# Products before copies in the token-major query units of a linear-attention and MLP kernel, with two buffer names changed

## The chip, the core and the metric

The kernel runs on one core of a Trainium2 chip. The metric is device time in microseconds (us) for one execution, the median of several. Five engines take part, each with its own instruction stream that it works off in order: TensorE (PE, with its weight loads as PEld), VectorE (DVE), ScalarE (ACT), GpSimd (POOL) and SyncE (SP, which issues the DMAs here).

## What is computed

Linear attention over 8 batches of 8 heads (576 tokens, 64 dimensions, 128 features), then a two-layer MLP over all 4608 tokens:

```python
def phi(x):
    proj = x @ w_phi                                  # 64 -> 128
    proj = proj - max(abs(proj), axis=-1)
    return concat([exp(proj), exp(-proj)], axis=-1)   # 256 features
kv  = phi(k).T @ v
z   = sum(phi(k), over tokens)
num = phi(q) @ kv
den = phi(q) @ z + 1e-6
x   = num / den                  # per head; heads side by side: 4608 x 512
h   = x @ w_in                   # 512 -> 2048
out = max(0.01 * h, h) @ w_out   # 2048 -> 512
```

## The kernel before

**Pairs.** Two heads are worked on together: 32 pairs, four for each batch. Pairs 0 to 3 (batch 0) go through `first_k_phase` and `first_q_phase` at the start. All others are a stream, `attention()`, in which the key phase of pair i (`k_phase`) alternates with the query phase of pair i-1: `token_q_phase` for pairs 4 to 7 (batch 1) and `q_phase` from pair 8 on.

**A token-major query unit.** A unit is up to 256 tokens of a pair (`units`: 256, 256 and 64). `q_group` (pairs 4 to 7, 12 units) and the inner loop of `first_q_phase` (nine units) do the same: PE projects the queries, DVE takes the largest magnitude and subtracts it, PE transposes the result, and ACT takes two exponentials (L322 and L323, in the first units L523 and L524). Then, for each of the two heads j, PE multiplies with the key-value sums (L328, L538) and ACT copies the numerator to `ring` (L330, L541) and the denominator plus 1e-6 to `dn` (L331, L542). DVE transposes `dn`, inverts it and transposes it back, and POOL multiplies. [...] A product is two matrix instructions, and the profile shows each f32 instruction of this kind as two records: so four instructions and eight records per unit of 256 tokens.

**Buffers.** `st(shape, type, tag)` takes a tile from a pool in which each tag has one buffer, or two for the tags in `BUFS` (`eq` among them). Who asks next for a tag in the program gets the buffer when the one before has been released. The key-value sums of a pair (`kvh`, L282 to L284) are copied by ACT out of the PSUM tile of tag `c`, of which there is one.

**Weights.** `load_weights` brings the MLP's weights in 32 pieces (w_in and w_out for each of 16 slices of the hidden layer, 512 KB each) through two staging buffers. For each piece: DMA, ACT L159, DVE L160, L161, L162, ACT L164 (into the scratch tile `cr`, whose tag is `kvl`), DVE L165, ACT rounds it (L68, `w0h` or `w1h`), DVE subtracts (L73, `w0l` or `w1l`). The stage's buffer is free for the next DMA when L162 and L164 have read it. From pair 8 on the tag `kvl` also holds the low part of the key-value sums.

**MLP.** Blocks of 256 tokens, 18 of them, each with 16 slices: `layer1` (12 matrix instructions of 256 columns, L590, L591, L593) and `layer2` (six of 512 columns, L609 to L611), in pure f32r, three products for one. The slices of block 0 come while the weights are still being made.

**The order.** Nothing of it is written by hand. Every instruction carries a priority from its place in the source, and a scheduler with an estimate of times sorts each engine's instructions ahead of the run. The key phases and units are generators, so that the stream goes on between two slices. A small edit can so change the order on all engines.

Of the kernel before, what the change touches and what calls it, by code (L numbers as in the profile page):

```python
# [9 lines left out]
F32 = mybir.dt.float32  # L10
# [3 lines left out]
AF = mybir.ActivationFunctionType  # L14
# [3 lines left out]
P = 128  # L18
B, H, S, D = 8, 8, 576, 64
NP = H // 2  # L20
F = 128
U = 288
DM = 512
# [22 lines left out]
def attention_moe_kernel(ctx: ExitStack, tc: tile.TileContext, q, k, v, vt, w_phi, w_in, w_out, out):  # L46
    nc = tc.nc
# [7 lines left out]
    def st(shape, dt, tag):  # L55
        return sp.tile(shape, dt, tag=tag, name=tag, bufs=BUFS.get(tag, 1))
# [8 lines left out]
    def copy_(key, o, i):  # L65
        e = pick(key) or "a"
        if e == "a":
            nc.scalar.copy(o, i)  # L68
        else:
            (nc.vector if e == "v" else nc.gpsimd).tensor_copy(o, i)  # L70
# [4 lines left out]
    def pt(tag):  # L75
        return ps.tile([P, 512], F32, tag=tag, name=tag, bufs=PBUFS[tag])
# [113 lines left out]
    def k_phase(i):  # L190
# [22 lines left out]
        for g in range(3):  # L213
            w = 2 if g < 2 else 1
# [4 lines left out]
            if plain:  # L219
                pk = pt("a")  # L220
                for s in range(w):
                    t0 = (2 * g + s) * P if g < 2 else S - P
                    proj(pk, s, rk[:, t0 : t0 + P])
                pkv = pk[r, 0 : 256 * w].rearrange("p (a f) -> p a f", f=F)
            else:
                for s in range(w):
                    t0 = (2 * g + s) * P if g < 2 else S - P
# [5 lines left out]
                    x = pmk[r, 2 * s : 2 * s + 2]  # L233
# [45 lines left out]
            for t in range(2):  # L279
                nc.tensor.transpose(kvtv[:, j, t], kvs[:, j, t], ident[0:66, 0:66])  # L280
        if i < NN:
            kvh = st([P, 2, 2, P], F32, "kvh")  # L282
            nc.scalar.copy(kvh[:, :, :, 0:64], kvtv[:, :, :, 0:64])
            nc.scalar.copy(kvh[:, :, :, 64:P], kvtv[:, :, :, 64:65].broadcast_to([P, 2, 2, 64]))  # L284
            kvs_of[i] = kvh, None
        else:
            kvh = st([P, 2, 2, P], F32R, "kvh")
            kvl = st([P, 2, 2, P], F32R, "kvl")
            zb = kvtv[:, :, :, 64:65].broadcast_to([P, 2, 2, 64])
            copy_("kvh", kvh[:, :, :, 0:64], kvtv[:, :, :, 0:64])  # L290
            copy_("kvh", kvh[:, :, :, 64:P], zb)
            nc.vector.tensor_tensor(kvl[:, :, :, 0:64], kvtv[:, :, :, 0:64], kvh[:, :, :, 0:64].bitcast(F32), op=ALU.subtract)
            nc.vector.tensor_tensor(kvl[:, :, :, 64:P], zb, kvh[:, :, :, 64:P].bitcast(F32), op=ALU.subtract)
            kvs_of[i] = kvh, kvl
# [5 lines left out]
    def proj(pk, s, x, n=P):  # L300
        nc.tensor.matmul(pk[0:n, 256 * s : 256 * s + 256], lhsT=x, rhs=bd, start=True, stop=True)  # L301

    def q_group(rq, t0, w, kvh, x, pm, dn):
        pq = pt("a")
        ns = max(w // P, 1)
        n = min(w, P)
        for s in range(ns):
            c = slice(t0 + s * P, t0 + s * P + n)
            proj(pq, s, rq[:, c], n)
        m4 = st([P, 4], F32, "m4")  # L310
        pqv = pq[0:n, 0 : 256 * ns].rearrange("p (a f) -> p a f", f=F)
        nc.vector.tensor_reduce(m4[0:n, 0 : 2 * ns], pqv, axis=AX.X, op=ALU.max, apply_absolute_value=True)
        nc.vector.tensor_tensor(pm[0:n, 0 : 2 * ns], pqv,
                                m4[0:n, 0 : 2 * ns].unsqueeze(2).broadcast_to([n, 2 * ns, F]), op=ALU.subtract)
        yield
        tr = pt("a")[:, 0 : 2 * w].rearrange("p (j t) -> p j t", j=2)
        for s in range(ns):
            for j in range(2):
                nc.tensor.transpose(tr[:, j, s * P : s * P + n], pm[0:n, 2 * s + j], ident[0:n, 0:n])
        ee = [st([P, 2, U], F32, "eq").rearrange("p a b -> p (a b)")[:, 0 : 2 * w].rearrange("p (j t) -> p j t", j=2)  # L320
              for t in range(2)]
        nc.scalar.activation(ee[0], tr, AF.Exp)  # L322
        nc.scalar.activation(ee[1], tr, AF.Exp, scale=-1.0)  # L323
        yield
        nm = pt("a")[:, 0 : 2 * w].rearrange("p (j t) -> p j t", j=2)
        for j in range(2):
            for t in range(2):
                nc.tensor.matmul(nm[:, j], lhsT=kvh[:, j, t], rhs=ee[t][:, j], start=t == 0, stop=t == 1)  # L328
            rr = slice(64 * j, 64 * j + 64)
            nc.scalar.copy(x[rr], nm[0:64, j])  # L330
            nc.scalar.activation(dn[rr], nm[64:128, j], AF.Copy, bias=1e-6)  # L331
        yield
        dt = st([P, U], F32, "mb")[:, 0:w]
        nc.vector.transpose(dt, dn)
        rc = st([P, 9], F32, "rc")[:, 0 : w // 32]
        nc.vector.reciprocal(rc, dt.rearrange("p (a c) -> p a c", c=32)[:, :, 0])
        nc.vector.transpose(dt.rearrange("p (a c) -> p a c", c=32), rc.unsqueeze(2).broadcast_to([P, w // 32, 32]))
        tt_("x", x, x, dt, ALU.mult)
        yield

    def token_q_phase(i):
        b, hp = divmod(i, NP)
        rq = qraw.pop(i)
        if i + 1 < B * NP:
            load_q(i + 1)
        tq = st([P, 2, 2, U], F32, "tq").rearrange("p a b c -> p a (b c)")
        for g, (t0, w) in enumerate(units):
            yield from q_group(rq, t0, w, kvs_of[i][0], ring[:, b % 2, hp, t0 : t0 + w],
                               tq[:, g % 2, 0:DM].rearrange("p (a f) -> p a f", f=F), st([P, U], F32, "dn")[:, 0:w])

    def q_phase(i):
        b, hp = divmod(i, NP)
# [141 lines left out]
    def first_q_phase(u):  # L494
        t0, w = units[u]
        rq = first_q[u]
        tail = u == 2
        if tail:
            rq = rq.rearrange("p a t -> p (a t)").unsqueeze(1)
            w = NP * w  # L500
        n, ns = P, 2
        for hp in range(1 if tail else NP):
            pq = pt("a" if u else "acc")
            for s in range(ns):
                proj(pq, s, rq[:, hp, s * P : s * P + n], n)
            m4 = st([P, 4], F32, "m4")
            pqv = pq[0:n, 0 : 256 * ns].rearrange("p (a f) -> p a f", f=F)
            nc.vector.tensor_reduce(m4[0:n, 0 : 2 * ns], pqv, axis=AX.X, op=ALU.max, apply_absolute_value=True)
            pm = st([P, 4, F], F32, "ek" if hp % 2 else "pmk")
            nc.vector.tensor_tensor(pm[0:n, 0 : 2 * ns], pqv,  # L510
                                    m4[0:n, 0 : 2 * ns].unsqueeze(2).broadcast_to([n, 2 * ns, F]), op=ALU.subtract)
            yield
            tr = pt("a")[:, 0 : 2 * w].rearrange("p (j t) -> p j t", j=2)
            for s in range(ns):
                for j in range(2):
                    nc.tensor.transpose(tr[:, j, s * P : s * P + n], pm[0:n, 2 * s + j], ident[0:n, 0:n])
            if hp % 2:
                ee = st([P, 2, S], F32, "qs")
                ee = [ee[:, t, 0 : 2 * w] for t in range(2)]
            else:  # L520
                ee = [st([P, 2, U], F32, "eq").rearrange("p a b -> p (a b)")[:, 0 : 2 * w] for t in range(2)]
            ee = [x.rearrange("p (j t) -> p j t", j=2) for x in ee]
            nc.scalar.activation(ee[0], tr, AF.Exp)  # L523
            nc.scalar.activation(ee[1], tr, AF.Exp, scale=-1.0)  # L524
            yield
            nm = pt("c" if u else "h")[:, 0 : 2 * w].rearrange("p (j t) -> p j t", j=2)
            dn = st([P, U], F32, "dn")[:, 0:w]
            x = ring[:, 0, :, t0:S] if tail else ring[:, 0, hp : hp + 1, t0 : t0 + w]
            m = x.shape[1]

            def heads(y):
                return y.rearrange("p (a t) -> p a t", a=m)

            for j in range(2):
                for h in range(m):
                    ts = slice(w // m * h, w // m * h + w // m)
                    for t in range(2):
                        nc.tensor.matmul(nm[:, j, ts], lhsT=kvs_of[hp + h][0][:, j, t], rhs=ee[t][:, j, ts],  # L538
                                         start=t == 0, stop=t == 1)
                rr = slice(64 * j, 64 * j + 64)  # L540
                nc.scalar.copy(x[rr], heads(nm[0:64, j]))  # L541
                nc.scalar.activation(dn[rr], nm[64:128, j], AF.Copy, bias=1e-6)  # L542
            yield
            dt = st([P, U], F32, "mb")[:, 0:w]
            nc.vector.transpose(dt, dn)
            rc = st([P, 9], F32, "rc")[:, 0 : w // 32]
            nc.vector.reciprocal(rc, dt.rearrange("p (a c) -> p a c", c=32)[:, :, 0])
            nc.vector.transpose(dt.rearrange("p (a c) -> p a c", c=32), rc.unsqueeze(2).broadcast_to([P, w // 32, 32]))  # L548
            tt_("x", x, x, heads(dt), ALU.mult)
            yield  # L550
# [145 lines left out]
```

## Time and profile before

Three runs gave 1200.81, 1201.39 and 1203.37 us, median 1201.39. The profiled execution took 1198.47 us, of which the trace spans 1196.7.

| stretch, us from the start | what runs | PE busy | DVE busy | ACT busy | POOL busy |
|---|---|---|---|---|---|
| 0 to 36 | first loads, key phases of pairs 0 to 3 | 30.80 | 22.30 | 21.69 | 1.45 |
| 36 to 164 | weights, first units, pairs 4 and 5, block 0 | 115.55 | 120.32 | 109.34 | 13.98 |
| 164 to 246 | pairs 5 to 8, block 1 | 82.00 | 43.14 | 49.21 | 21.04 |
| 246 to 500 | attention of batches 2 and on, MLP | 249.08 | 174.22 | 192.16 | 117.54 |
| 500 to 1100 | the same | 597.95 | 384.03 | 436.64 | 260.81 |
| 1100 to 1197 | MLP alone | 90.40 | 15.48 | 25.96 | 2.83 |

The table is the view of stretches, put together. PE's busy time includes pipelined instructions that overlap, so what matters is how far apart they start. Idle time of an engine that isn't the one waited for costs nothing.

### The profile page before, as it was taken

The numbers are of one execution on the slowest core, as the hardware profiler recorded it, in microseconds if no ns is written. First come the engines' busy times: TensorE is split into PE (matmuls) and PEld (weight loads), VectorE is DVE, ScalarE is ACT, GpSimd is POOL, SyncE is SP. The second block draws the span as 40 slices with busy tenths as digits, with TensorE's granted clock in tenths as the row PEclk, the third lists the DMA queues.
The fourth block names the chain that finished last, engine by engine and source line by source line (L and its number), as shares of the span: only waits on it lengthen the run. The fifth ranks groups of instructions, "written<-read, shape, count | busy, mean of one in ns | idle before, by whom it ended". The sixth has DMA issues, their size and how long they took to land.

```text
span 1196.7 us, 21180 instructions
## 1 busy us (share of the span) xinstructions
PE 1165.8 (97%) x7576; PEld 1041.0 (87%) x7576; DVE 759.5 (63%) x1508; ACT 835.0 (70%) x2104; POOL 417.7 (35%) x418
## 2 busy tenths in 40 slices
PE   8898999999999999999999999999999999999998
PEld 5577788889898989989999999998999999988987
DVE  5998974565777777677777777726777776111111
ACT  5887875676767788888888888837787877432222
POOL 0110011253535364544545455514454544110000
PEclk9999999999999999999999999999999999999999
DMA  7334521111101111011111111101111100000000
GB/s 209 106 116 148 158 86 43 42 49 32 48 22 41 41 35 46 11 49 32 50 31 50 32 50 32 39 22 32 29 50 31 50 1 19 1 19 19 1 19 18
DMA packets 62778, 57.01 MB, mean 48 GB/s; under 512 B 45136, under 2 KB 46288, under 8 KB 62672
## 3 DMA queue, kind: packets, MB, share of 16 engines
q1 hardware_dynamic: 62672, 55.65, 16.1%
q8 instruction: 60, 0.98, 0.3%
q14 instruction: 46, 0.38, 0.1%
HBM read 46.20 MB, written 9.44 MB: 46 GB/s over the span
## 4 chain that ended last, share of the span: by engine, by line
PE 83%; DVE 7%; ACT 4%; issue 2%; DMA 2%; POOL 1%; SPq 0%; DVEq 0%; ACTq 0%
PE h L590 10%; PE h L591 10%; PE h L593 10%; PE acc L609 10%; PE acc L610 10%; PE acc L611 10%; PE c L210 7%; PE a L409 2%; PE a L412 2%; PE a L410 2%; PE a L301 2%; PE a L230 2%; DMA qh<-in_w_out_dram 1%; PE a L328 1%; PE a L369 1%
## 5 line engine op out<-in xcount | busy, mean ns | idle before, releaser
L590 PE MATMUL h<-xh,w0h 128*128 128x256 f32 x1152 | 294.5, 285 | 5.1 <-DVE gl L598 3.4
L591 PE MATMUL h<-xh,w0l 128*128 128x256 f32 x1152 | 291.5, 283 | 1.4 <-DVE w0l L73 1.4
L598 DVE TENSOR_TENSOR gl<-h,gh 128x256 fp32r<-128x256 f32 x288 | 119.5, 418 | 244.5 <-ACT gh L68 230.9
L609 PE MATMUL acc<-w1h,gh 128*128 128x512 f32 x576 | 230.1, 400 | 3.1 <-ACT gh L68 3.0
L590 PEld LDWEIGHTS h<-xh,w0h 128*128 128x128 f32 x1152 | 218.0, 189 | 16.8 <-DVE gl L598 6.0
L610 PE MATMUL acc<-w1l,gh 128*128 128x512 f32 x576 | 228.0, 396 | 0.0
L591 PEld LDWEIGHTS h<-xh,w0l 128*128 128x128 f32 x1152 | 217.8, 189 | 8.6 <-DVE w0l L73 1.6
L596 ACT ACTIVATE h<-h 128x256 f32<-128x256 f32 x288 | 105.8, 369 | 158.4 <-PE h L593 155.4
L611 PE MATMUL acc<-w1h,gl 128*128 128x512 f32 x576 | 202.6, 396 | 0.0
L593 PE MATMUL h<-xl,w0h 128*128 128x256 f32 x1152 | 198.6, 282 | 0.6 <-POOL xl L73 0.6
L73 POOL TENSOR_TENSOR ql<-eq,qh 128x576 fp32r<-128x576 f32 x96 | 145.1, 1526 | 97.9 <-ACT qh L68 85.2
L593 PEld LDWEIGHTS h<-xl,w0h 128*128 128x128 f32 x1152 | 163.6, 189 | 1.6 <-POOL xl L73 0.9
L73 POOL TENSOR_TENSOR kpl<-ek,kph 128x512 fp32r<-128x512 f32 x72 | 96.7, 1343 | 138.3 <-ACT kph L68 71.1
L609 PEld LDWEIGHTS acc<-w1h,gh 128*128 128x128 f32 x576 | 108.5, 188 | 24.2 <-ACT gh L68 4.7
L68 ACT CAST gh<-h 128x256 fp32r<-128x256 f32 x288 | 105.6, 372 | 30.3 <-PE acc L610 25.9
L73 POOL TENSOR_TENSOR ring<-ring,mb 128x576 f32<-128x576 f32 (+2 forms) x45 | 50.7, 1127 | 213.6 <-DVE mb L548 50.3
L610 PEld LDWEIGHTS acc<-w1l,gh 128*128 128x128 f32 x576 | 108.6, 189 | 18.1
L73 POOL TENSOR_TENSOR xl<-ring,xh 128x256 fp32r<-128x256 f32 (+3 forms) x96 | 62.1, 679 | 150.8 <-PE h L593 129.4
L611 PEld LDWEIGHTS acc<-w1h,gl 128*128 128x128 f32 x576 | 98.9, 189 | 8.5
L248 ACT ACTIVATE ek<-pmk 128x256 f32<-128x256 f32 (+1 forms) x128 | 53.3, 417 | 33.6 <-POOL kpl L73 15.9
L210 PE MATMUL c<-kph,vh 128*66 128x256 f32 x240 | 62.4, 282 | 1.8 <-ACT kph L68 1.8
L198 DVE TENSOR_TENSOR ks<-rk,ks 64x576 fp32r<-64x576 f32 x40 | 43.1, 1078 | 30.6 <-ACT ks L68 29.8
(201 smaller groups left out, 2254.6 us busy)
## 6 DMA issues: line engine op xcount, KB each, us to landing
out_dram<-o SPq DMA_DIRECT2D x35, 256.0 KB, 2.1
rk<-in_k_dram SPq DMA_DIRECT2D x29, 288.0 KB, 2.8
ring<-in_w_in_dram SPq DMA_DIRECT2D x16, 512.0 KB, 3.4
qh<-in_w_out_dram SPq DMA_DIRECT2D x16, 512.0 KB, 3.5
rq<-in_q_dram SPq DMA_DIRECT2D x28, 288.0 KB, 3.0
rv<-in_v_dram SPq DMA_DIRECT2D x29, 256.0 KB, 3.4
rv<-in_vt_dram SPq DMA_DIRECT2D x58, 32.0 KB, 2.9
fr<-in_k_dram SPq DMA_DIRECT2D x2, 288.0 KB, 3.3
```

The lines of the kernel that those rows point to most:

```text
L68: nc.scalar.copy(o, i)
L73: (nc.vector if pick(key) == "v" else nc.gpsimd).tensor_tensor(o, a, b, op=op)
L210: nc.tensor.matmul(kvp[0 : lt.shape[1], 256 * j : 256 * j + 256], lhsT=lt, rhs=rt, start=first and j == 0, stop=last, skip_group_check=True)
L248: nc.scalar.activation(ek[r, :, 0:F], pmk[r, 2 * s : 2 * s + 2], AF.Exp)
L590: nc.tensor.matmul(ph, lhsT=weight(0, "h", ft)[:, d * P : d * P + P], rhs=xh[:, d], start=d == 0, stop=False)
L591: nc.tensor.matmul(ph, lhsT=weight(0, "l", ft)[:, d * P : d * P + P], rhs=xh[:, d], start=False, stop=False)
L593: nc.tensor.matmul(ph, lhsT=weight(0, "h", ft)[:, d * P : d * P + P], rhs=xl[:, d], start=False, stop=d == NP - 1)
L596: nc.scalar.activation(ph, ph, AF.Prelu, alpha=0.01)
L598: nc.vector.tensor_tensor(gl, ph, gh.bitcast(F32), op=ALU.subtract)
L609: nc.tensor.matmul(a, lhsT=gh[:, ts], rhs=weight(1, "h", ft), start=ft == 0, stop=False)
L610: nc.tensor.matmul(a, lhsT=gh[:, ts], rhs=weight(1, "l", ft), start=False, stop=False)
L611: nc.tensor.matmul(a, lhsT=gl[:, ts], rhs=weight(1, "h", ft), start=False, stop=ft == NFT - 1)
```

## The change

There are three edits. In both kinds of token-major unit all products of both heads are issued ahead of all four copies, and the denominators are copied first. The units of `token_q_phase` with an odd number take their exponentials from the tile of tag `qs` instead of `eq`. The odd pairs of batch 1 (5 and 7) hold their key-value sums in the buffer of tag `kvl` instead of `kvh`.

```diff
         if i < NN:
-            kvh = st([P, 2, 2, P], F32, "kvh")
+            kvh = st([P, 2, 2, P], F32, "kvl" if i % 2 else "kvh")
...
-    def q_group(rq, t0, w, kvh, x, pm, dn):
+    def q_group(rq, t0, w, kvh, x, pm, dn, od):
...
-        ee = [st([P, 2, U], F32, "eq").rearrange("p a b -> p (a b)")[:, 0 : 2 * w].rearrange("p (j t) -> p j t", j=2)
-              for t in range(2)]
+        if od:
+            ee = st([P, 2, S], F32, "qs")
+            ee = [ee[:, t, 0 : 2 * w] for t in range(2)]
+        else:
+            ee = [st([P, 2, U], F32, "eq").rearrange("p a b -> p (a b)")[:, 0 : 2 * w] for t in range(2)]
+        ee = [e.rearrange("p (j t) -> p j t", j=2) for e in ee]
...
         for j in range(2):
             for t in range(2):
                 nc.tensor.matmul(nm[:, j], lhsT=kvh[:, j, t], rhs=ee[t][:, j], start=t == 0, stop=t == 1)
+        for j in range(2):
+            rr = slice(64 * j, 64 * j + 64)
+            nc.scalar.activation(dn[rr], nm[64:128, j], AF.Copy, bias=1e-6)
+        for j in range(2):
             rr = slice(64 * j, 64 * j + 64)
             nc.scalar.copy(x[rr], nm[0:64, j])
-            nc.scalar.activation(dn[rr], nm[64:128, j], AF.Copy, bias=1e-6)
...
-                               tq[:, g % 2, 0:DM].rearrange("p (a f) -> p a f", f=F), st([P, U], F32, "dn")[:, 0:w])
+                               tq[:, g % 2, 0:DM].rearrange("p (a f) -> p a f", f=F), st([P, U], F32, "dn")[:, 0:w], g % 2)
...
+            for j in range(2):
+                rr = slice(64 * j, 64 * j + 64)
+                nc.scalar.activation(dn[rr], nm[64:128, j], AF.Copy, bias=1e-6)
             for j in range(2):
                 rr = slice(64 * j, 64 * j + 64)
                 nc.scalar.copy(x[rr], heads(nm[0:64, j]))
-                nc.scalar.activation(dn[rr], nm[64:128, j], AF.Copy, bias=1e-6)
```

The rows below are the program's order of instructions: line, operation, out<-in by tile names, size, and xN for N equal ones. From L320 on the lines of the changed kernel are shifted, by 10 at the end: L549 and L552 are L542 and L541 of before, L335 and L338 are L331 and L330, L606, L608 are L596, L598, and L600 to L621 are L590 to L611.

First, ACT at the first two units of batch 0, before:

```order
L541 COPY ring<-h 64x256
L542 ACTIVATE dn<-h 64x256
L473 COPY f_80<-c 128x4x64
L474 COPY f_80<-c 128x4x64
L541 COPY ring<-h 64x256
L68 CAST w1h_629<-ql 128x512
```

and the same place of the changed kernel:

```order
L549 ACTIVATE dn<-h 64x256 x2
L552 COPY ring<-h 64x256 x2
L480 COPY f_80<-c 128x4x64
L481 COPY f_80<-c 128x4x64
L68 CAST w1h_629<-ql 128x512
```

The four copies of a unit now stand together, where other work used to stand between those of the first and the second head.

Second, ACT at the key-value sums of pair 5 (L283, L284). Before, they stand between the 27th and the 28th of the 32 L164 (`w0h_892` and `w1h_905` are the weights of slices 12 to 15):

```order
L159 ACTIVATE ql<-qh 128x512
L330 COPY ring<-a 64x64
L331 ACTIVATE dn<-a 64x64
L68 CAST w0h_892<-ql 128x512
L283 COPY kvh<-c 128x4x64
L284 COPY kvh<-c 128x4x64
L330 COPY ring<-a 64x64
L331 ACTIVATE dn<-a 64x64
L164 ACTIVATE kvl<-qh 128x512
```

In the changed kernel, from the second-last piece on:

```order
L159 ACTIVATE ql<-ring 128x512
L68 CAST w1h_905<-ql 128x512
L164 ACTIVATE kvl<-ring 128x512
L606 ACTIVATE h<-h 128x256
L68 CAST gh<-h 128x256
L159 ACTIVATE ql<-qh 128x512
L68 CAST w0h_892<-ql 128x512
L164 ACTIVATE kvl<-qh 128x512
L68 CAST xh<-ring 128x256 x4
L283 COPY kvl<-c 128x4x64
L284 COPY kvl<-c 128x4x64
```

They moved behind the last L164 of all, since the scratch tiles of all 32 pieces ask for tag `kvl` earlier in the program. Ahead of that there are only weights and the MLP's own steps.

Third, PE between two slices of block 0 near the end of the weights, before (the last six instructions of layer 2 for one slice, then layer 1 of the last slice):

```order
L611 MATMUL acc<-w1h_905,gl 128x512 x2
L328 MATMUL a<-eq,kvh 128x256 x2
L301 MATMUL a<-bd,rq 64x256
L590 MATMUL h<-xh,w0h_892 128x256
L328 MATMUL a<-eq,kvh 128x256 x2
L591 MATMUL h<-xh,w0l_893 128x256
```

and in the changed kernel, between the same kinds of steps:

```order
L621 MATMUL acc<-w1h_905,gl 128x512 x2
L600 MATMUL h<-xh,w0h_892 128x256
L601 MATMUL h<-xh,w0l_893 128x256
L600 MATMUL h<-xh,w0h_892 128x256
L601 MATMUL h<-xh,w0l_893 128x256
```

The attention's products (L328) and projections (L301) are gone from this place. They stand behind the last slice of block 0. On DVE, at the same place, before:

```order
L165 ISA ql<-ql,kvl 128x1024
L160 TENSOR_SCALAR ql<-ql 128x512
L161 TENSOR_SCALAR ql<-ql 128x512
L238 TENSOR_REDUCE m_1273<-a 128x4
L73 TENSOR_TENSOR w0l_893<-ql,w0h_892 128x512
L162 SCALAR_TENSOR_TENSOR ql<-qh,ql 128x512
L241 TENSOR_TENSOR pmk<-a,m_1273 128x512
L312 TENSOR_REDUCE m_1295<-a 128x4
L165 ISA ql<-ql,kvl 128x1024
```

and in the changed kernel:

```order
L165 ISA ql<-ql,kvl 128x1024
L160 TENSOR_SCALAR ql<-ql 128x512
L161 TENSOR_SCALAR ql<-ql 128x512
L73 TENSOR_TENSOR w1l_906<-ql,w1h_905 128x512
L162 SCALAR_TENSOR_TENSOR ql<-ring,ql 128x512
L608 TENSOR_TENSOR gl<-h,gh 128x256
L165 ISA ql<-ql,kvl 128x1024
```

From the 23rd L165 to the 32nd only the five steps of a weight piece and the MLP's L608 are left. Counted in the order: ahead of the 23rd L165 stand 17 attention instructions more than before (two each of L238, L241, L312 and L313, three each of the two `dn` transposes and the reciprocal) and one `gl` more; ahead of the 31st stand five less (one each of L238, L241, L312, L313 and the first transpose), ahead of the 32nd ten less. Ahead of layer 1 of the last slice of block 0, PE has 20 f32 matrix instructions of 256 columns (eight L210, six L301, six L328) and four transposes (L319) less than before. From about block 8 of the MLP on, PE's work stands in the same order in both kernels.

More of the change, by code (lines that the diff above doesn't have):

```diff
@@ L539, in first_q_phase @@
                                          start=t == 0, stop=t == 1)
+            for j in range(2):
+                rr = slice(64 * j, 64 * j + 64)
+                nc.scalar.activation(dn[rr], nm[64:128, j], AF.Copy, bias=1e-6)
+            for j in range(2):
                 rr = slice(64 * j, 64 * j + 64)
                 nc.scalar.copy(x[rr], heads(nm[0:64, j]))
-                nc.scalar.activation(dn[rr], nm[64:128, j], AF.Copy, bias=1e-6)
             yield
```

## The prediction

> **What bounds the kernel now.** On the page PE is busy for 97% of the span, which doesn't say where it is the limit. So I read the stretches next, then DVE and PE in order of time where the weights end.
>
> ```profile
> 36.00:164.00 128.00, 115.55 (x621) 91.53 (x619) 120.32 (x246) 109.34 (x246) 13.98 (x19) 0.97 0.44 132
> 164.00:246.00 82.00, 82.00 (x504) 70.62 (x504) 43.14 (x94) 49.21 (x138) 21.04 (x31) 1.00 0.17 46
> 246.00:500.00 254.00, 249.08 (x1690) 227.32 (x1689) 174.22 (x335) 192.16 (x488) 117.54 (x106) 1.00 0.13 37
> 500.00:1100.00 600.00, 597.95 (x4064) 549.20 (x4063) 384.03 (x762) 436.64 (x1119) 260.81 (x245) 1.00 0.11 31
> ```
>
> A row of stretches gives its length, then PE, PEld, DVE, ACT and POOL busy. From 164 us on PE is busy without a break (82.00 of 82.00, 597.95 of 600.00): there the time is PE's work, and the change takes none of that away. From 36 to 164 us it is the other way round: DVE is busy for 120.32 of 128 us, PE has 12.45 us visibly idle. In that stretch DVE makes the weights. So the span is the time at which PE stops waiting for weights, plus the PE work that is left at that time, plus small losses. **Two numbers decide: when the last weights come, and how much PE has done by then.**
>
> ```profile
> L165 DVE CUSTOM_DVE_ANT_0 ql<-ql,kvl x32: 646/684/1209, 26.5 to 163.4; 128x1024 uint16<-128x1024 uint16 x32
> ...
> 121.32 0.68 DVE L162 SCALAR_TENSOR_TENSOR ql<-qh,ql 128x512 int32<-128x512 int32 x1
> 121.92 0.68 DVE L312 TENSOR_REDUCE m<-a 128x4 f32<-128x512 f32 x1
> 122.52 0.42 DVE L160 TENSOR_SCALAR ql<-ql 128x512 f32<-128x512 f32 x1
> 122.85 0.69 DVE L165 CUSTOM_DVE_ANT_0 ql<-ql,kvl 128x1024 uint16<-128x1024 uint16 x1
> 123.45 0.69 DVE L313 TENSOR_TENSOR tq<-a,m 128x512 f32<-128x512 f32 x1
> 124.05 0.42 DVE L161 TENSOR_SCALAR ql<-ql 128x512 int32<-128x512 int32 x1
> 124.39 0.69 DVE L73 TENSOR_TENSOR w1l<-ql,w1h 128x512 fp32r<-128x512 f32 x1
> 124.99 0.68 DVE L162 SCALAR_TENSOR_TENSOR ql<-ring,ql 128x512 int32<-128x512 int32 x1
> 125.81 0.69 DVE L165 CUSTOM_DVE_ANT_0 ql<-ql,kvl 128x1024 uint16<-128x1024 uint16 x1
> ...
> 158.85 0.67 DVE L165 CUSTOM_DVE_ANT_0 ql<-ql,kvl 128x1024 uint16<-128x1024 uint16 x1
> ...
> 163.37 0.67 DVE L165 CUSTOM_DVE_ANT_0 ql<-ql,kvl 128x1024 uint16<-128x1024 uint16 x1
> ```
>
> L165 is one step of each of the 32 pieces. The ones at 125.81, 158.85 and 163.37 are the 23rd, 31st and 32nd (start and duration in us). DVE runs one instruction behind the other; 0.68 long, they start 0.60 apart. Layer 1 of the last slice of block 0 needs the 31st piece.
>
> ```profile
> 161.54 0.39 PE L590 MATMUL h<-xh,w0h 128*128 128x256 f32 x1
> ```
>
> It starts at 161.54, or 2.7 us after that piece's L165. What PE is doing while it waits is attention of pairs 4 and 5.
>
> **The change, part by part.** *Products before copies.* It removes the wait of PE for the copies of the first head.
>
> ```profile
>   ACT dn L542: 9.9, 11
> ...
>   ACT dn L331: 1.7, 4
> ...
> DVE ql L160 <- ACT ql L159: 1.9, 4, 0.8
> DVE w1l L73 <- ACT w1h L68: 1.6, 2, 1.0
> DVE ql L165 <- ACT kvl L164: 1.0, 1, 1.0
> DVE mb L545 <- ACT dn L542: 0.4, 1, 0.4
> DVE mb L334 <- ACT dn L331: 0.3, 1, 0.3
> ```
>
> The first two rows are what PE sat idle ahead of the products L538 and L328 until the copy of `dn` was done: 11.6 us in 15 waits. All of it lies ahead of 164 us, where DVE is the bound. The other rows are DVE's own waits from 36 to 134 us. Those on `dn` make 0.7 us, all five 5.2. So of the 11.6 us only what DVE got out of it can shorten the stretch: from 0 to 5.2 us. I take 1.3, twice the 0.7, since a unit done sooner also spares a part of the others.
>
> *Exponentials of odd units in `qs`.* No row of PE or ACT shows a wait for a buffer of `eq` in units of batch 1; it is taken at nothing, within the same 0 to 5.2 us. No instruction is added by any of the three edits.
>
> *Sums of odd pairs in `kvl`.* This one moves work. By the order, pair 5's sums go into `kvl` only behind the last L164, since the 32 scratch tiles have that buffer first. Until then its products can't start, the one PSUM tile of tag `c` stays full, and the keys of pair 6 can't be summed either. **From the 23rd piece to the 31st PE's queue holds the MLP and nothing else.**
>
> *When the weights come.* Ahead of the 23rd L165 DVE now has 17 attention instructions and one `gl` more. By the rows they are four of 0.68 and four that are partly half size (4.4 us for the eight), three groups of 0.45, 0.19 and 0.44 (2.8, by the rows below) and 0.4: 7.6 us, and as they start closer together than they are long, some 7.0.
>
> ```profile
> 158.17 0.45 DVE L334 STREAM_TRANSPOSE mb<-dn 128x256 f32<-128x256 f32 x1
> ...
> 159.77 0.20 DVE L336 RECIPROCAL rc<-mb 128x8 f32<-128x8 f32 x1
> ...
> 160.80 0.44 DVE L337 STREAM_TRANSPOSE mb<-rc 128x256 f32<-128x256 f32 x1
> ```
>
> So the 23rd comes at 125.8 + 7.0 - 1.3 = 131.5. From there to the 31st are eight pieces without attention. DVE alone needs 0.60 + 0.33 + 0.34 + 0.60 + 0.60 by the starts above, with half a `gl` 2.64 us for a piece. But each staging buffer must be read, filled and read again:
>
> ```profile
> 80.63 4.85 DMA qh<-in_w_out_dram
> ...
> 122.06 3.44 DMA qh<-in_w_out_dram
> ...
> 125.59 0.69 ACT ql L159
> ```
>
> From the end of one L162 (122.0) to the next of the same buffer: 3.44 for the DMA, 0.8 to the end of L159, 0.67 for L160 and L161, 0.6 for L73 of the other piece and 0.7 for L162, 6.3 us for two pieces, 3.15 for one. With the DMA of 4.85 it is 3.85. I take 3.2, next to the quicker DMA, as little else is loaded then. Eight times 3.2 are 25.6: the 31st L165 at 157.1, layer 1 of the last slice at 159.8, or **1.7 us earlier than before.**
>
> *What PE has done by then.* By the order it has 20 f32 instructions and four transposes less behind it.
>
> ```profile
> 155.27 0.86 PE a L328 x4
> ...
> 113.07 0.60 PE L319 MATMUL a<-ident,tq 128*128 128x128 f32 x4
> ...
> 82.34 0.28 PE L590 MATMUL h<-xh,w0h 128*128 128x256 f32 x1
> 82.46 0.28 PE L591 MATMUL h<-xh,w0l 128*128 128x256 f32 x1
> ...
> 92.67 0.40 PE L611 MATMUL acc<-w1h,gl 128*128 128x512 f32 x1
> 92.91 0.40 PE L609 MATMUL acc<-w1h,gh 128*128 128x512 f32 x1
> ```
>
> Four records are two instructions, so one takes 0.43: 8.6 us, and 0.5 for the transposes, **9.1 us of PE work that is still to be done.** It fits the other way round too: a slice of the MLP is 12 starts 0.12 apart and six 0.23 apart, 2.8 us, while its two pieces take 6.4. PE so stands idle for 3.6 us a slice, over some four slices.
>
> *Behind that.* PE is full from then on in both kernels, and the order becomes the same about block 8. The visible losses of 246 to 500 us (4.9) may go or double; taken at no change.
>
> *Sum.* 9.1 - 1.7 = 7.4 us more. The profiled execution took 1198.47 us, of which 1196.7 are the span: 1205.9. The median of the runs shown is 1201.39, 2.9 above it, so 1208.8 for the median, and all times below are made against it.
>
> **The rivals.** *DVE runs through (faster).* Place: 36 us to the 31st piece. If DVE loses none of the 7.7 us that it is idle in 128 (all put ahead of the 23rd piece) and a piece takes 2.64 us, the 31st L165 comes at 125.8 + 7.0 - 7.7 + 8 x 2.64 = 146.2, 12.6 earlier; 9.1 are owed, so 3.5 faster: 1197.9. It decides from 149.7 on, where the debt is just paid. For it: DVE is at 94% there. Against it: both must hold in full, and the staging rows give 3.15.
>
> *The debt is repaid.* The attention held back gives PE more to do behind 164 us, and the 4.9 us of losses go: 7.4 - 4.9 = 2.5, at 1203.9; with the waits on top, within 0.2%. Against it: those losses lie in other phases, up to 500 us.
>
> *Half clock.* The clock granted to PE fell between 93 and 121 us:
>
> ```profile
> L596 ACT ACTIVATE h<-h 128x256 f32<-128x256 f32 x288 | 105.8, 369 | 158.4 <-PE h L593 155.4
> ...
> 49.00:52.40 3.40, 1.93 (x9) 1.26 (x9) 3.40 (x8) 3.01 (x7) 1.16 (x2) 1.00 0.45 135
> ...
> 113.90:117.30 3.40, 1.18 (x6) 1.06 (x6) 1.77 (x5) 3.40 (x10) 0.00 (x0) 1.00 0.84 221
> 117.30:120.70 3.40, 3.40 (x9) 2.49 (x8) 2.87 (x6) 2.61 (x6) 0.00 (x0) 0.50 0.54 166
> ```
>
> The last number but two in a row is the granted clock. Behind 3.4 us in which PE was busy for 1.18 the clock is 0.50 for 3.4 us; behind 1.93 it isn't. In the new stretch PE works 2.8 of 6.4 us, so some windows fall below. Mostly that is hidden: 5.6 us at half clock still fit into 6.4. But DVE's `gl` stands 3.1 us behind the subtraction that releases layer 1; layer 1 at half clock with two ACT steps like L596 (0.37) takes 3.6. Half a us for each of some four slices and 1.7 for the last window are 3.7 us more: 1212.5.
>
> [...]
>
> *The change doesn't do what it says.* Then nothing changes, some 1201 us. The order speaks against it: all copies stand together.
>
> **How the numbers follow.** Forecast, slower by some 7: 0.58. Half clock on top: 0.07. Repaid, or no effect: 0.17. DVE runs through: 0.18. This kernel's measurement can tell about 0.2% (2.4 us) from no change. Faster 0.18, same 0.17, slower 0.65. The forecast's own bounds are 2.64 and 3.85 for a piece (minus 4.5 and plus 5.2 us) and 0 to 5.2 for the waits (plus 1.3, minus 3.9). With the two neighbours at 1197.9 and 1212.5 the range is 1198 to 1215.
>
> **What would show it.** Right: PE with idle of about 3 us a slice between some 130 and 160 us, ended by DVE's `w0l`; pair 5's copies (L283) behind the last L164; PE's waits for `dn` nearly gone; behind 165 us no new idle. Wrong: a last L165 ahead of 150 us, PE busy with attention among the last slices, or less idle than 4.9 us from 246 to 500.

## The result, and the profile after

The changed kernel takes 1215.54 us (median of 4 runs, 1214.39 to 1216.07), the kernel before in the same series 1202.38 (1200.81 to 1203.58). The ratio is 1.0116, with a 95% interval from 1.0104 to 1.0127: 13.2 us slower, where 7.4 had been forecast, and half a microsecond above the range. Of the 6.7 us between the forecast of 1208.8 and the result, 1.0 is the kernel before, which took 1202.38 in this series and not 1201.39. The profiled execution of the changed kernel took 1216.07 us, of which the trace spans 1214.3.

First the view of stretches of the changed kernel, with the same bounds and columns as in the prediction:

```profile
36.00:164.00 128.00, 109.26 (x571) 88.63 (x569) 116.48 (x237) 103.33 (x229) 13.11 (x18) 0.92 0.45 128
164.00:246.00 82.00, 81.96 (x491) 70.01 (x492) 30.72 (x70) 43.85 (x124) 15.93 (x25) 1.00 0.13 34
246.00:500.00 254.00, 247.51 (x1660) 225.40 (x1659) 183.02 (x356) 193.19 (x488) 115.32 (x108) 0.99 0.15 42
500.00:1100.00 600.00, 594.82 (x4053) 546.67 (x4052) 391.31 (x769) 442.62 (x1136) 262.64 (x247) 1.00 0.11 31
```

PE's visible idle time grew from 12.45 to 18.7 us in the first row. But it also grew behind 246 us, from 4.9 to 6.5 and from 2.0 to 5.2 us, where the forecast had no change. Next, what PE waited for from 36 to 165 us (engine, line, releaser: us in all, times, longest):

```profile
PE acc L619 <- ACT gh L68: 8.4, 7, 1.9
PE h L545 <- ACT eq L530: 3.8, 1, 3.8
PE h L601 <- DVE w0l L73: 2.2, 5, 0.6
PE a L319 <- ACT kph L249: 1.7, 1, 1.7
PE h L600 <- ACT w0h L68: 1.6, 3, 0.7
PE c L545 <- ACT qs L530: 1.1, 1, 1.1
```

No wait for `dn` is left, as the first edit intends. In its place PE waits for the MLP's own steps, since nothing else stands in its queue. The end of the weights, from the timelines of DVE (23rd, 31st and 32nd L165), of PE (layer 1 of the last slice of block 0) and of ACT (the sums of pair 5):

```profile
134.84 0.68 DVE L165 CUSTOM_DVE_ANT_0 ql<-ql,kvl 128x1024 uint16<-128x1024 uint16 x1
...
160.99 0.68 DVE L165 CUSTOM_DVE_ANT_0 ql<-ql,kvl 128x1024 uint16<-128x1024 uint16 x1
...
164.72 0.69 DVE L165 CUSTOM_DVE_ANT_0 ql<-ql,kvl 128x1024 uint16<-128x1024 uint16 x1
```

```profile
163.02 0.38 PE L600 MATMUL h<-xh,w0h 128*128 128x256 f32 x1 [0.72 <-ACT w0h L68]
```

```profile
165.75 0.36 ACT L283 COPY kvl<-c 128x256 f32<-128x256 f32 x1
```

Pair 5's copy stands 1.0 us behind the start of the last L165. Eight pieces took 160.99 - 134.84 = 26.15 us, 3.27 each (forecast 3.2). Layer 1 of the last slice started at 163.02, 1.5 us later than in the trace of before, where 1.7 earlier had been forecast. From the 23rd L165 to there, first the changed kernel, then before:

```profile
134.84:163.02 28.18, 19.85 (x77) 14.48 (x76) 24.10 (x48) 18.32 (x36) 0.00 (x0) 0.76 0.54 149
...
125.81:161.54 35.73, 33.54 (x181) 25.41 (x178) 34.31 (x74) 31.89 (x74) 2.37 (x5) 1.00 0.51 153
```

**A ledger of PE.** To see where the rest was lost, the start of layer 1 of each slice is set against the PE work that the order puts ahead of it (by the distance of their starts in the trace of before: 0.117 us for an f32r instruction of 256 columns and 0.23 for one of 512, as from 502.81 to 504.44 us, 0.131 for 288, as at 501.63, 0.434 for an f32 instruction of 256, as L328 at 155.11, and 0.11 for a transpose of 128, as L319 at 113.07; some 1129 us in all, the same in every kernel here). Start minus work is what PE has lost by then. "Before again" is the profiled execution of the run e11_hold_alone below, whose order on PE, DVE and ACT is that of before up to slice 94: up to there, a second execution of the same order.

| lost by slice, us | 16 | 64 | 68 | 96 | 120 | 164 | 284 |
|---|---|---|---|---|---|---|---|
| before | 34.0 | 44.2 | 46.0 | 49.0 | 50.7 | 52.8 | 63.4 |
| before again | 37.9 | 48.1 | 49.9 | 52.7 | 54.2 | 56.2 | 67.2 |
| after | 45.0 | 51.6 | 59.7 | 62.8 | 68.3 | 70.3 | 81.0 |

Two executions of one order differ by 3.9 us by slice 16, and what each loses behind it agrees within 0.5. The change cost 7.1 to 11.0 us by slice 16 (forecast 7.4). From slice 16 to 64 it got 3.6 back. **In block 4, slices 64 to 67, it lost 8.1 us where before loses 1.8, and from slice 96 to 120 another 5.5 where before loses 1.7.** From slice 16 to the end it loses 36.0 us and before 29.4: 6.6 us more, and that is the part that the forecast lacks. What happens in block 4 is shown by the stretch from layer 1 of slice 64 to that of slice 68, first before:

```profile
376.99:393.30 16.31, 15.73 (x102) 13.71 (x101) 9.98 (x20) 13.67 (x38) 10.43 (x12) 1.00 0.20 69
```

and in the changed kernel, whole and in windows of 3.41 us:

```profile
378.68:403.86 25.18, 20.77 (x126) 17.97 (x125) 21.30 (x42) 18.64 (x48) 10.43 (x12) 0.93 0.20 58
```

```profile
383.70:387.11 3.41, 2.95 (x20) 2.41 (x19) 2.28 (x5) 3.24 (x9) 0.61 (x1) 1.00 0.39 146
387.11:390.52 3.41, 1.04 (x5) 0.78 (x6) 3.28 (x8) 0.47 (x2) 1.30 (x1) 1.00 0.01 4
390.52:393.94 3.42, 3.42 (x16) 3.11 (x16) 3.36 (x7) 1.64 (x3) 0.57 (x2) 0.50 0.19 73
393.94:397.35 3.41, 2.28 (x17) 1.84 (x16) 3.25 (x7) 3.06 (x9) 1.59 (x2) 1.00 0.11 20
```

Its timelines of PE and of ACT there:

```profile
387.84 0.40 PE L376 MATMUL a<-qs,wq 128*128 128x288 f32 x1 [1.13 <-DVE tq L378]
...
390.01 0.40 PE L376 MATMUL a<-qs,wq 128*128 128x288 f32 x1 [1.65 <-DVE pmk L235]
...
391.01 0.58 PE L600 MATMUL h<-xh,w0h 128*128 128x256 f32 x1
...
396.50 0.50 PE L619 MATMUL acc<-w1h,gh 128*128 128x512 f32 x1 [1.13 <-ACT gh L68]
```

```profile
390.66 0.30 ACT L68 CAST xh<-ring 128x128 fp32r<-128x128 f32 x1 [3.08 <-POOL ring L73]
```

Block 4 holds tokens 1024 to 1279, and from 1152 on they belong to batch 2. So it is the first block that needs pairs 8 to 11. ACT waits 3.08 us for the last of their products in `ring`, PE's queue has only attention ahead of it, and that waits for DVE. Behind a window with 1.04 us of PE work the clock is 0.50 for the next 3.4 us. Before, these pairs are done in time and the same stretch takes 16.31 us.

### The profile page after: what moved, and what is told of

It is laid out like the page before. It is cut to its first block, busy times and chain, and to the rows that moved or that the text cites. A ratio compares the mean times of both kernels' runs of the same rounds, so it can differ in the third digit from the quotient of the medians.

```text
span 1214.3 us, 21177 instructions
## 1 busy us (share of the span) xinstructions
PE 1172.1 (97%) x7576; PEld 1048.8 (86%) x7576; DVE 760.0 (63%) x1508; ACT 834.7 (69%) x2104; POOL 414.1 (34%) x418
## 4 chain that ended last, share of the span: by engine, by line
PE 82%; DVE 7%; ACT 5%; DMA 3%; issue 2%; SPq 0%; POOL 0%; ACTq 0%; DVEq 0%; POOLq 0%
PE h L600 10%; PE h L603 10%; PE h L601 10%; PE acc L619 10%; PE acc L620 10%; PE acc L621 10%; PE c L210 7%; PE a L301 2%; PE a L417 2%; PE a L416 2%; PE a L419 2%; PE a L230 2%; DMA ring<-in_w_in_dram 2%; PE a L332 1%; PE a L376 1%
## 5 line engine op out<-in xcount | busy, mean ns | idle before, releaser
L600 PE MATMUL h<-xh,w0h 128*128 128x256 f32 x1152 | 296.3, 287 | 5.2 <-DVE gl L608 3.5
L608 DVE TENSOR_TENSOR gl<-h,gh 128x256 fp32r<-128x256 f32 x288 | 119.0, 417 | 242.2 <-ACT gh L68 220.1
L600 PEld LDWEIGHTS h<-xh,w0h 128*128 128x128 f32 x1152 | 219.1, 190 | 17.1 <-DVE gl L608 6.0
L606 ACT ACTIVATE h<-h 128x256 f32<-128x256 f32 x288 | 105.5, 368 | 158.7 <-PE h L603 156.7
L621 PE MATMUL acc<-w1h,gl 128*128 128x512 f32 x576 | 205.5, 398 | 0.0
L603 PE MATMUL h<-xl,w0h 128*128 128x256 f32 x1152 | 201.2, 283 | 0.0
L73 POOL TENSOR_TENSOR xl<-ring,xh 128x256 fp32r<-128x256 f32 (+3 forms) x96 | 59.2, 647 | 182.2 <-PE h L603 160.2
L621 PEld LDWEIGHTS acc<-w1h,gl 128*128 128x128 f32 x576 | 100.3, 190 | 8.8
L248 ACT ACTIVATE ek<-pmk 128x256 f32<-128x256 f32 (+1 forms) x128 | 53.4, 417 | 30.6 <-POOL kpl L73 16.2
L210 PE MATMUL c<-kph,vh 128*66 128x256 f32 x240 | 62.4, 282 | 2.1 <-DVE kvl L293 1.4
```

The lines of the kernel that those rows point to most:

```text
L73: (nc.vector if pick(key) == "v" else nc.gpsimd).tensor_tensor(o, a, b, op=op)
L210: nc.tensor.matmul(kvp[0 : lt.shape[1], 256 * j : 256 * j + 256], lhsT=lt, rhs=rt, start=first and j == 0, stop=last, skip_group_check=True)
L248: nc.scalar.activation(ek[r, :, 0:F], pmk[r, 2 * s : 2 * s + 2], AF.Exp)
L600: nc.tensor.matmul(ph, lhsT=weight(0, "h", ft)[:, d * P : d * P + P], rhs=xh[:, d], start=d == 0, stop=False)
L603: nc.tensor.matmul(ph, lhsT=weight(0, "h", ft)[:, d * P : d * P + P], rhs=xl[:, d], start=False, stop=d == NP - 1)
L606: nc.scalar.activation(ph, ph, AF.Prelu, alpha=0.01)
```

## The experiments

The letters stand for these theories. A: sharing `kvl` with the weights' scratch makes the loss in block 0. B: the new order inside the units is itself the loss. D: the attention that is behind at slice 64 is made up in a crowd at the start of block 4, and PE waits there along its chain. S: products before copies gains early, and gives it back because the attention stands ahead of its place later. Where an expectation words its theory, its own words hold. Each diff is against the kernel named in its heading.

**1. The change without its third edit** (against after).

```diff
-            kvh = st([P, 2, 2, P], F32, "kvl" if i % 2 else "kvh")
+            kvh = st([P, 2, 2, P], F32, "kvh")
```

> The changed kernel with its third edit undone: the sums of all pairs go into the buffer of kvh again; products first and the exponentials in qs stay. Theory A (the shared buffer holds pair 5's attention back until the weights are done): by the order pair 5's sums stand behind the 22nd L164 again, and PE has 142.8 us of work behind it at layer 1 of the last slice of block 0 (119.0 in the changed kernel, 128.1 before), while DVE has about 10 us more ahead of the 31st piece than before. So about 5 us faster than before, some 1197 us, no MLP-only stretch. Rival B (the earlier attention that products-first brings delays the weights, and that is what costs): still 1209 or more.

Measured: 1203.85 us against 1201.36, ratio 1.0024 (1.0015 to 1.0034). 2.5 us are left of the 13.2, so the third edit makes most of the loss. But theory A's 1197 is missed: the two others don't gain, they cost 0.2%.

**2. The third edit alone** (against before).

```diff
-            kvh = st([P, 2, 2, P], F32, "kvh")
+            kvh = st([P, 2, 2, P], F32, "kvl" if i % 2 else "kvh")
```

> The kernel before with the third edit alone. Theory A: the MLP-only stretch comes with it (from the 27th piece on), PE has 119.0 us of work behind it at layer 1 of the last slice, 9.1 less than before, the pieces come at most some 2 us sooner: 7 us slower or more, 1208 to 1216. Rival B: within 2 us of before, 1200 to 1204.

Measured: 1211.21 us, ratio 1.0085 (1.0069 to 1.01), as A expects. In its trace the clock is full from 36 to 164 us, and layer 1 of the last slice of block 0 starts 1.5 us earlier than before, with the 9.1 us of PE work still owed:

```profile
36.00:164.00 128.00, 106.45 (x584) 82.90 (x583) 117.52 (x238) 105.44 (x235) 13.67 (x19) 1.00 0.45 128
...
160.06 0.38 PE L590 MATMUL h<-xh,w0h 128*128 128x256 f32 x1
```

**3. A buffer of its own for the odd pairs** (against after; tag `kvo` has no other user).

```diff
-            kvh = st([P, 2, 2, P], F32, "kvl" if i % 2 else "kvh")
+            kvh = st([P, 2, 2, P], F32, "kvo" if i % 2 else "kvh")
```

> The changed kernel with the sums of the odd pairs in a buffer of their own, that no other tile uses. Theory A (it is the sharing with the weights' scratch, not a second buffer for the sums): as with the third edit undone, 1194 to 1200 us. Rival B: 1209 or more. If a second buffer itself did harm: between the two.

Measured: 1208.88 us, ratio 1.0065 (1.005 to 1.008). A miss. The total would fit rival B, or harm by a second buffer itself, but the early part speaks against both: by the ledger it has lost 29.5 us by slice 16 and 36.5 by slice 64, 4.5 and 7.7 less than before. From slice 80 to 164 it then loses 22.3 where before loses 6.1. Room in the buffers alone gains where it was meant to, and more is lost behind.

**4. Products before copies alone** (before with the first edit in both kinds of unit, as in the change).

> The kernel before with the first edit alone: products first, denominators copied first. By the order it is the same as the changed kernel without the third edit but for 24 lines on PE, so the exponentials' buffer does nothing: within 2 us of that kernel. Theory A: some 1197 us. Rival B: 1209 or more.

Measured: 1203.84 us, ratio 1.0022 (1.0013 to 1.0032), the same as run 1, and not theory A's 1197. So the exponentials in `qs` do nothing. By the ledger it is 2.6 us ahead of before by slice 16 and 4.1 by slice 64, loses 1.0 in block 4, and from slice 80 to 164 loses 16.2 us.

**5 and 6. Only pair 5, only pair 7 in the shared buffer** (against after).

```diff
-            kvh = st([P, 2, 2, P], F32, "kvl" if i % 2 else "kvh")
+            kvh = st([P, 2, 2, P], F32, "kvl" if i == 5 else "kvh")
...
+            kvh = st([P, 2, 2, P], F32, "kvl" if i == 7 else "kvh")
```

> The changed kernel with only pair 5 in the buffer of kvl (pair 7 back in kvh). By the order PE has 119.0 us of work behind it at layer 1 of the last slice of block 0, as in the changed kernel, and from the middle of block 4 on its order is that of before. Theory A (pair 5 behind the weights' scratch): PE has lost some 10 us more than before by the end of block 0. For the second loss, of some 6 us in block 4 and 4 in blocks 6 and 7 of the changed kernel, theory D (attention held back comes due where block 4 first needs batch 2) expects the loss in block 4 again, since PE is 6.4 us of attention behind there too, and none in blocks 6 and 7: 1209 to 1214. Theory O (all of it is the order of blocks 4 to 7, which differs from before by accident): no loss in block 4 beyond before's 2 us: 1205 to 1209.

> The changed kernel with only pair 7 in the buffer of kvl. When pair 7 comes, the weights are done. Theory A: no MLP-only stretch, PE as far as with the third edit undone (142.8 us at the last slice), PE's loss by the end of block 0 at or below before's 34. The time as with the third edit undone or with an own buffer, 1203 to 1209; a theory in which any use of kvl by the sums costs expects 1212 or more.

Measured: pair 5 alone 1211.44 us, ratio 1.0093 (1.0072 to 1.0113), with 44.1 us lost by slice 16 and 11.3 in block 4. Pair 7 alone 1205.99, ratio 1.0042 (1.0029 to 1.0055), with 29.8 by slice 16 and 2.6 in block 4. Pair 5 is the one that waits behind the weights.

**7. Products first in the nine units of batch 0 alone** (before with the first edit in `first_q_phase` only).

> The kernel before with products first in the units of batch 0 alone. By the order PE is 12.5 us further at the last slice than before, and in blocks 7 to 10 the attention stands 5 us earlier against the MLP than before, as in the kernels with own buffer or without the third edit. Theory S (products first wins some 4 us in the early part, and this other steady order gives back some 2 us in each of blocks 6 to 10): loss by the end of block 0 some 2 us below before's 34, 8 to 12 us given back between blocks 6 and 10: 1202 to 1208. If products first cost something of its own each time, the loss would be in the early part.

Measured: 1207.11 us, ratio 1.0051 (1.0035 to 1.0066), but with 35.9 us lost by slice 16, no gain that can be told from the 34.0 and 37.9 of before, and 10.9 from slice 120 to 164. The total fits and the account of the early part doesn't: it comes ahead of before only by slice 64, by some 3 us.

**8. Run 4 with the attention held back during pair 8** (it gets the MLP's priority there).

```diff
     def advance(goal):
+        if 8 <= state["n"] < 9:
+            while state["n"] < goal:
+                state["n"] = max(state["n"], next(stream, B * NP))
+            return
```

> Products first alone, with the attention's instructions that are recorded while pair 8 is the latest at the MLP's priority instead of their own, which sets the attention back by 7.6 us of PE work in block 1 and makes the order of blocks 7 to 10 close to that of before (548.8, 581.4 and 612.5 us of PE work at the starts of slices 120, 128 and 136; before 549.7, 581.1 and 612.3). Theory S: the early gain of some 4 us stays and blocks 6 to 10 lose no more than before: 1196 to 1200. If the early gain of products first has to be given back in any order: 1202 or more.

Measured: 1204.92 us, ratio 1.0037 (1.0024 to 1.0051). A miss: the early gain lasts to slice 96, but 6.3 us are lost in slices 96 to 99, and 6.8 us at half clock lie there (510.52 to 517.35 us; the mean clock of the whole execution is 0.994, in run 4 0.997). From slice 120 to 164 it loses 4.2 us, run 4 9.4.

**9. All three edits, with only pair 7 in `kvl`, and the attention held in slices 96 to 103** (against run 6; `state["s"]` is the slice).

```diff
     def advance(goal):
+        if 96 <= state["s"] < 104:
+            while state["n"] < goal:
+                state["n"] = max(state["n"], next(stream, B * NP))
+            return
```

> Of all three edits, with the buffer of tag kvl for pair 7 alone (as in the run of pair 7, 1205.99 us), and the attention held at the MLP's priority during slices 96 to 103. By the order it then stands from slice 104 to 160 within about 1.2 us of PE work of the place that it has before the change, not 4 to 6 us ahead of it. Theory S (the early gain is given back because the attention stands ahead of its place in blocks 6 to 10, where the waits at each block's start cost 1 us each): the early gain stays and from slice 120 to 164 about 2 to 4 us are lost (before 2.1, pair 7 alone 11.0): 1196 to 1200 us. Rival (the loss does not hang on the place of the attention but on the order inside the units): 8 us or more lost from 120 to 164, and 1203 us or more.

Measured: 1196.71 us (1196.36 to 1198.37) against 1201.05, ratio 0.9968 (0.9956 to 0.9981): **faster than both kernels.** From slice 120 to 164 it loses 2.6 us where run 6 loses 10.9. The stretch between layer 1 of these two slices in run 6, then its waits:

```profile
602.60:783.10 180.50, 176.04 (x1188) 159.52 (x1188) 134.14 (x247) 138.69 (x349) 86.05 (x76) 1.00 0.14 39
```

```profile
PE h L600 <- DVE gl L608: 1.4, 2, 0.7
PE c L210 <- DVE kvl L293: 0.9, 1, 0.9
PE h L603 <- POOL xl L73: 0.6, 2, 0.3
```

and in this run, where the view of waits has no entry at all for it:

```profile
599.40:774.60 175.20, 175.18 (x1209) 161.91 (x1208) 130.27 (x250) 145.12 (x368) 92.38 (x79) 1.00 0.14 38
```

PE has 4.5 us visibly idle in the one and none in the other.

**10. Products first in the 12 units of pairs 4 to 7 alone** (before with the first edit in `q_group` only).

> Products before copies in the 12 units of pairs 4 to 7 alone; first units, exponentials and key-value sums as before. By the order PE's work stands within 1.5 us of its place before, through the whole program. Of the waits for dn only those of L328 (1.7 us in 4) can go. Theory S: no shift, so nothing lost later: 1198 to 1202 us, within 0.2% of before. Rival (the edit of the units costs by itself, whatever stands where): 1203 us or more, with losses from slice 120 to 164 well above the 2.1 of before.

Measured: 1211.89 us, ratio 1.0089 (1.0075 to 1.0103). This run speaks against S as it was put. PE's work stands within 0.5 us of its place before at slices 104 and 112 (though 3.7 off at slice 100), in run 9 within 0.5 and 1.2, and still 8.6 us go from slice 120 to 164:

```profile
PE c L210 <- POOL kpl L73: 2.0, 3, 1.0
PE h L593 <- DVE gl L601: 1.1, 2, 0.9
PE a L412 <- ACT qh L68: 1.1, 2, 0.8
```

Query products of one pair (L412 and its neighbours) and key sums of the next (L210) wait there for what POOL, DVE and ACT have to make of the projections, and two gaps between slices hold half of the loss (2.4 us behind slice 129, 2.0 behind slice 161). That both kinds stand in the same gap doesn't explain it: of the 44 gaps, 15 hold both in this run, but 13 do before and 18 in run 9. So how far ahead the attention stands isn't enough to tell the loss, and what else decides isn't shown. The rival of this run, that the edit costs by itself, falls with run 9, which has the edit and not the loss.

**11. The hold alone** (before with the edit of run 9 to `advance`).

> The kernel before with nothing but the hold of slices 96 to 103 (the attention at the MLP's priority there). A control for the run of 1196.71 us: by the order PE's work stands within 0.6 us of its place before. If the gain of that run is the products' early gain, kept because the later losses are gone: this one is at 1199 to 1203 us, within 0.2% of before. Rival (the hold gains by itself): 1198 us or less.

Measured: 1200.22 us against 1200.88, ratio 0.9992 (0.9983 to 1.0001). The hold alone gains nothing that can be told from none, so the gain of run 9 needs the edits too.

**12. A debt made by hand** (run 4, with the attention recorded in slices 24 to 39 put far behind the MLP).

```diff
     def advance(goal):
+        if 24 <= state["s"] < 40:
+            tc.cur_priority += 1500
+            while state["n"] < goal:
+                state["n"] = max(state["n"], next(stream, B * NP))
+            tc.cur_priority -= 1500
+            return
```

> Products before copies alone, no buffer shared, no other edit of before; but the attention recorded during slices 24 to 39 gets a priority far behind the MLP's. By the order 16.1 us of PE work less than before stand ahead of slice 64 (after the change it is 5.7), and they come between slices 64 and 66; from slice 68 on the order is that of before within 2 us. Theory D (the attention that is behind at slice 64 has to be made up in a crowd at the start of block 4, where PE waits along its chain, and this costs what it costs whichever edit made the debt): 8 us or more lost from slice 64 to 68 (before 1.8, after the change 8.1), and 1203 us or more, though the stretch ahead is faster than before. Rival (the loss in block 4 comes of the shared buffer or of its clock alone): 3 us or less lost there, and 1196 to 1200 us.

Measured: 1223.75 us, ratio 1.019 (1.0176 to 1.0204). It is ahead of before up to slice 64 (37.3 us lost against 44.2), loses 34.9 us from there to slice 68, and from slice 80 on loses as little as before. No buffer is shared in it. The stretch from slice 64 to 68, its largest waits, and two windows of it:

```profile
354.00:418.40 64.40, 47.78 (x226) 38.35 (x225) 43.23 (x83) 46.92 (x113) 32.49 (x29) 0.71 0.14 41
```

```profile
PE c L210 <- ACT kph L68: 6.9, 4, 2.4
PE h L599 <- ACT xh L68: 2.3, 1, 2.3
PE a L418 <- POOL ql L73: 1.4, 2, 1.0
```

```profile
382.04:385.45 3.41, 1.57 (x6) 1.01 (x6) 2.38 (x5) 1.65 (x5) 1.56 (x1) 0.50 0.00 0
385.45:388.87 3.42, 1.52 (x8) 1.29 (x7) 1.35 (x2) 3.24 (x8) 0.69 (x1) 0.50 0.00 0
```

No engine is busy for more than 47.78 of 64.40 us: much of PE's work is pairs of the attention with no MLP slice between their steps, and PE waits for each hand-over. Its clock is down to 0.71 on average.

## Why the forecast was right in sign and short in size

The runs side by side at block 4. "Crowd" is the PE work that the order puts between layer 1 of slice 64 and that of slice 66. The last column counts the windows of 3.41 us in which the clock was 0.50:

| kernel | PE work ahead of slice 64, against before | crowd, us | lost from slice 64 to 68, us | windows at half clock |
|---|---|---|---|---|
| before (11 alike) | 0 | 4.9 | 1.8 | 0 |
| held back (8) | 0 | 4.9 | 3.9 | 1 |
| products alone (4; 1 alike) | +6.7 | 6.4 | 1.0 | 0 |
| first units alone (7) | +3.9 | 7.2 | 2.5 | 0 |
| pair 7 alone (6; 9 alike) | +3.9 | 7.5 | 2.6 | 0 |
| third edit alone (2) | -2.6 | 7.7 | 4.3 | 0 |
| units of pairs 4 to 7 alone (10) | +0.7 | 9.1 | 4.1 | 1 |
| own buffer (3) | +2.1 | 9.3 | 2.6 | 0 |
| after | -5.7 | 10.8 | 8.1 | 1 |
| pair 5 alone (5) | -6.4 | 12.2 | 11.3 | 3 |
| debt by hand (12) | -16.1 | 21.9 | 34.9 | 11 |

Up to a crowd of 9.3 us the loss is 1.0 to 4.3 us in no clear order; beyond it, it grows steeply. The half clock has a part in it. In the changed kernel f32r instructions of 256 columns start 0.21 us apart behind 392.25 us, at half clock, instead of 0.117, so a window of 3.41 us at half clock costs some 1.7 us at most (an estimate: half of 3.41, as the clock was 0.50). That is 1.7 of the 6.3 us that the changed kernel loses here beyond before, and 18.8 of the 33.1 in run 12: the clock alone makes neither.

- **What bounds the kernel.** Up to the end of the weights the reading held. "Plus small losses" did not: behind 164 us the losses depend on when the attention falls due.
- **Products before copies (1.3 us, 0 to 5.2).** The waits are gone, and run 4 is 2.6 us ahead of before by slice 16. That alone would be within the scatter of 3.9, but all seven runs with this edit in both kinds of unit and pair 5 out of `kvl` (1, 3, 4, 6, 8, 9 and 12) have lost some 29 to 32 us by then, against 34.0 and 37.9. Alone it still ends 2.5 us slower. The forecast priced the waits that go and not the order that comes. Its 11.6 us in 15 waits are also misread: the rows add PE's own waits (4.2) to those of its weight loads, PEld, that lie beside them. The sum goes by DVE's rows, so nothing hangs on it.
- **Exponentials in `qs` (nothing).** Right: runs 1 and 4 differ by 0.01 us.
- **Sums in `kvl`.** The mechanism is shown by runs 1, 2, 5 and 6: pair 5, behind the last L164. The 23rd piece came at 134.84 (forecast 131.5), the next eight took 26.15 us (25.6). Layer 1 of the last slice was 1.5 us late instead of 1.7 early, a term off by 3.2 us, within the 3.9 by which two executions of the order of before differ. PE's debt of 9.1 us is in the order. So 7.4 stands beside 7.1 to 11.0 measured. Run 2, with the same debt and the full clock, has that layer 1 1.5 us early. The prediction's cross-check of the debt doesn't come out: 3.6 us of idle time in each of four slices are 14.4 us, not 9.1, and what PE was visibly idle there is 8.3 us (28.18 - 19.85), where before it was 2.2.
- **The step that failed: "Behind that... taken at no change."** The order did become the same by about block 8. But pairs 8 to 11, held back with pair 5, came due at block 4 in a crowd, for 6.3 us more than before. Run 12 makes such a crowd without any shared buffer and loses 34.9 us there, with 11 windows at half clock, so it is the debt and not the buffer. Only the 3.6 us repaid ahead of it had been thought of, as a rival. Another 3.8 us went from slice 96 to 120 (5.5 against 1.7). They come with the order there and not with the debt: run 2, whose PE order there is the changed kernel's instruction by instruction, loses 5.5 too; run 5, with the debt but the PE order of before, 1.8; runs 11 and 12, close to the order of before, 1.5 and 2.1; every other run 3.4 or more. What in the order costs them isn't shown.
- **The rivals.** DVE didn't run through: the last L165 came at 164.72. Half the clock did come: from 134.5 to 137.9 us, from 148.18 to 158.42 and at 390.52, and also from about 49 to 56, far ahead of the new stretch. Its price in the changed kernel was not measured by itself, since it stands there behind windows in which PE was also idle (busy for 0.37, 1.02, 1.54 and 1.04 of some 3.4 us, from 45.78, 131.11, 144.77 and 387.11 us). Run 2, at the full clock, has lost some 42 us by slice 16, 3 less than the changed kernel, so the early loss comes for the most part without it.
- **What would show it.** PE's idle time among the last slices was there, but ended mostly by ACT's `gh` (8.4 us) and less by DVE's `w0l` (2.2). "No new idle behind 165 us" was the sign that came out wrong.

**Open:** what in the order of blocks 6 to 10 costs runs 1, 3, 4, 6, 7 and 10 from 8.6 to 11.0 us between slices 120 and 164, and run 8 4.2, where before, the changed kernel and runs 2, 5, 11 and 12 lose 2.0 to 2.1 and run 9 loses 2.6. Run 10 rules out that the distance from the place of before decides alone, and the count of gaps that hold both L210 and L412 doesn't tell the runs apart. In runs 1, 3, 4, 6 and 7 two gaps hold over a third of it: 2.0 us behind slice 147 and 1.7 behind slice 160 in each of them.

## What to carry to other kernels

When an edit holds work back, the account doesn't end where the bounding engine is full again: look for the next point at which the held-back work is needed, and price it there as a chain with nothing to hide it. Where a scheduler orders the program, a wait removed is also a new order for everything behind, so compare the order through the whole program, and try to keep the gain by putting the later order back, as run 9 did (run 10 shows that the place of the held-back work alone doesn't decide). One profiled execution is one sample: here the same order differed by 3.9 us by slice 16.

## What the runs showed of the hardware

How busy PE was in the windows of 3.41 us ahead of a half clock and ahead of a full one. In the changed kernel around 150 us:

```profile
144.77:148.18 3.41, 1.54 (x9) 1.17 (x8) 3.10 (x7) 2.52 (x6) 0.00 (x0) 1.00 0.54 154
148.18:151.59 3.41, 2.97 (x10) 1.97 (x9) 2.60 (x6) 1.85 (x4) 0.00 (x0) 0.50 0.57 154
151.59:155.00 3.41, 2.44 (x10) 1.95 (x9) 3.31 (x7) 2.25 (x5) 0.00 (x0) 0.50 0.57 156
```

A window with 1.54 us of PE work was followed by one at 0.50, and so were the next two, themselves at 0.50, with 2.97 and 2.44 us. The one behind them, with 3.18 us, was followed by the full clock:

```profile
155.00:158.42 3.42, 3.18 (x11) 2.34 (x10) 2.54 (x6) 2.25 (x4) 0.00 (x0) 0.50 0.56 153
158.42:161.83 3.41, 2.12 (x13) 1.75 (x13) 3.22 (x7) 2.07 (x6) 0.00 (x0) 1.00 0.57 156
```

In run 12 the half clock so lasted for seven windows on end, from 368.39 to 392.28 us. The window ahead of them has 2.34 us of work:

```profile
364.98:368.39 3.41, 2.34 (x16) 1.72 (x14) 0.00 (x0) 3.31 (x8) 2.62 (x4) 1.00 0.00 0
368.39:371.80 3.41, 2.55 (x8) 1.51 (x7) 2.00 (x5) 1.83 (x6) 1.08 (x2) 0.50 0.43 96
```

In the changed kernel the window with 2.28 us of work (from 393.94, above) was followed by the full clock:

```profile
397.40:403.86 6.46, 6.46 (x44) 5.85 (x43) 6.22 (x16) 5.28 (x16) 2.48 (x4) 1.00 0.33 87
```

The trace of before shows, at a place that the prediction leaves out, the half clock behind a window with 2.40 us of work, more than the 1.93 behind which the clock stayed full there:

```profile
93.40:96.80 3.40, 2.40 (x20) 2.03 (x19) 2.65 (x8) 3.27 (x8) 0.00 (x0) 1.00 0.52 154
96.80:100.20 3.40, 3.40 (x15) 3.21 (x15) 3.33 (x8) 2.66 (x6) 0.73 (x1) 0.50 0.52 161
```

So the busy time of a window, as the profile shows it, doesn't tell the clock of the next one. At full clock, 1.93 and 2.28 us were followed by 1.00, but 2.34 and 2.40 by 0.50. At half clock, the 3.18 us above were followed by 1.00, but 3.22 in run 12 (399.11 to 402.52 us) by 0.50.
